# Turning 48 of the attention matrices by DVE squares and DMAs through DRAM instead of by PE

## The chip, the cores and the metric

The kernel runs on one core of a Trainium2 chip. The core has a matrix engine (PE; its weight loads are listed as PEld), a vector engine (DVE), an activation engine (ACT), a general engine (POOL), and a queue engine (SP) that here only issues DMAs. DMAs run on 16 DMA engines. The engines work in parallel, each in the order of its own instruction stream, and wait for each other on semaphores. The metric is the time of one execution on the device in microseconds (us), lower is better; the median of several runs is given.

## What is computed

Attention that keeps the 32 largest scores of each row, then an MLP with exact GELU on its output, all in float32:

```python
B, H, S, D = 8, 8, 576, 64
scores = scale * np.matmul(q, k.transpose(0, 1, 3, 2))          # (B, H, S, S)
kth = np.partition(scores, -32, axis=-1)[..., -32:-31]
scores = np.where(scores >= kth, scores, -1e9)
attn = np.exp(scores - scores.max(-1, keepdims=True))
attn = attn / (attn.sum(-1, keepdims=True) + 1e-9)              # P
x = np.matmul(attn, v)                                          # then (B*S, H*D) = (4608, 512)
h = x @ w_in                                                    # (4608, 2048)
g = 0.5 * h * (1.0 + erf(h / sqrt(2)))
return g @ w_out                                                # (4608, 512)
```

## The kernel before

**Items.** The heads are taken in pairs: 8 batches with 4 pairs each. An item is 128 query rows of one pair of heads (both heads side by side, `e` = 0 and 1), or, for the 64 rows left over at the end of a sequence, the last rows of two pairs (`t == NM`, a last-row item). Each batch has 16 main items and 2 last-row items, so there are N = 144. Main items come in twos: an even item and the odd one behind it are neighbouring 128-row tiles of the same pair of heads. Two batches make a ring of 36 items.

**The tile of an item.** `S_of[i]` is a 128 x 1152 tile, called s in the profile: 576 keys of head 0 and 576 keys of head 1. Its columns are ordered as 4 blocks of 128 keys of head 0, the last 64 keys of head 0 and those of head 1 next to each other, and 4 blocks of 128 keys of head 1: nine blocks of 128. Scores, the mask, the exponentials and the normalised P all live in this tile, one after the other. There are six such buffers.

**The loop.** The main loop runs a step n for each item and works on several items at once. In step n:

- PE computes scores (L371) and keys' ends (`last_keys`, L334) of items ahead; ACT copies them to s (L379, L342).
- PE multiplies P of the item pair that is finished with v (`attend(n - 3)`, L654, only when n - 3 is odd, since it takes 256 columns: an even item and the odd one behind it). ACT copies the result to xT (L659).
- PE turns over P of item n - 2 (`transposes(n - 2)`): one transpose for the 64 + 64 last keys (`tails`, L562) and eight for the blocks of both heads (`both`, `turn_over`, L592); ACT copies these to the tile pt (L572, L606).
- Between all these, PE runs pieces of the MLP of tokens that are ready (`mlp`: L712 is the first layer, L800 to L856 the second). `left[0]` says how many pieces a step gets.
- ACT applies mask and exponential to item n - 1 (`softmax`, L500 and L512), with the table loads that a change between GELU and exp needs, and GELU to the MLP's first layer (L728).
- DVE finds the 32nd largest score of each row of item n (`top_k`): four rounds of MAX8 and MATCH_REPLACE8. Rounds 0 and 1 run over 288 columns (the larger of two halves), rounds 2 and 3 over 576. The last thing in the step is the reciprocal of the sums of item n - 1 (`inverse`, L487).
- POOL prepares the lists for the top-k (L432, L440), adds the small constant to the sums (L493), multiplies P of item n - 1 by the reciprocals (`normalise`, L535) and adds up parts of the MLP.

An even step has the scores of two items, `attend` and an even item's transposes; an odd step has an odd item's transposes. From item 9 on P is normalised in place by POOL (`DIAGS`); before that PE multiplies by a diagonal matrix as it transposes.

**The tile pt.** It is one buffer of 128 keys x 9 blocks x 256 columns. Columns 0 to 127 hold the turned P of the even item, 128 to 255 that of the odd item. In the kernel before, blocks 0 to 3 are head 0, 4 to 7 head 1, and 8 the last keys of both.

**Queues.** SP's instruction stream holds the loads of q and k (L109, for pairs from the second batch's on 8 DMAs per load, in runs of 32 columns, so that DVE can turn them over in 32 x 32 squares, L269 to L273), the loads of v (L116, L119) and the stores of the output (`store`, L779). A DMA that has to wait holds up all DMAs behind it on SP. DMAs that read or write the raw tiles wait for the engine that uses them.

**An order written out by hand.** The scheduler is off (`manual_schedule`): the order of each engine's instructions is the order in which the loop issues them. The lines around the change:

```python
product = attend(n - 3)
...
tr = transposes(n - 2)
...
if few[0]:
    now, tr, prep = tr + prep[:1], [], prep[1:]
for x, piece in enumerate(now):
    piece(n + 2 if few[0] else None)
    ready[0] = n_tok[0]
    if few[0] and x == 2:
        break
    mlp(1)
```

`few[0]` holds from step 13 on. `SINGLE` is range(18, 28): items whose top-k runs all rounds over 576 columns, since POOL is busy with the weights then.

Of the kernel before, what the change touches and what calls it, by code (L numbers as in the profile page):

```python
# [8 lines left out]
TOPK = 32  # L9
# [5 lines left out]
def kernel(  # L15
# [19 lines left out]
    nc = tc.nc  # L35
# [5 lines left out]
    B, H, S, D = q.shape  # L41
# [19 lines left out]

    const = ctx.enter_context(tc.tile_pool(name="const", bufs=1))
    work = ctx.enter_context(tc.tile_pool(name="work", bufs=2))
    ps = ctx.enter_context(tc.tile_pool(name="ps", bufs=2, space=bass.MemoryType.PSUM))
    ctx.enter_context(tc.manual_schedule())

# [24 lines left out]
    def raw_of(n, pair):  # L91
        if n != "v":
            return raws[n][pair % 2 if pair < SQUARES else 0]
        return raws[n][pair % len(raws[n])]

    def load(n, pair, queue=None, queue2=None):
        if pair >= n_pairs:
# [341 lines left out]
            both, top = lists_of[i][:, :, 1].bitcast(i32), lists_of[i][:, :, 0].bitcast(i32)  # L439
            nc.gpsimd.tensor_tensor(into_of(i)[:, :, 1].bitcast(i32), both, top, op=ALU.subtract)  # L440

    def top_k(i, last):


        stat_of[i] = st = {
            "first": work.tile([P, 2, 8], f32, tag="first", name="first"),
            "neg": work.tile([P, 2], f32, tag="neg", name="neg"),
            "bias": work.tile([P, 2], f32, tag="bias", name="bias"),
            "den": work.tile([P, 2], f32, tag="den", name="den"),
            "rden": work.tile([P, 2], f32, tag="rden", name="rden"),  # L450
        }
        top = work.tile([P, 2, TOPK - 8], f32, tag="top", bufs=1, name="top")
        into = [st["first"]] + [top[:, :, 8 * r : 8 * r + 8] for r in range(TOPK // 8 - 1)]
        if paired(i):
            t = lists_of[i]
            u = into_of(i)
            both = u.rearrange("p e h n -> p e (h n)")
            rounds = [(t[:, :, 0], u[:, :, 0]), (u[:, :, 0], u[:, :, 0])]
            rounds = [(*(rounds[r] if 16 * r < TOPK else (both, both)), x) for r, x in enumerate(into)]
        else:  # L460
            s = S_of[i].rearrange("p (e n) -> p e n", e=2)
            t = work.tile([P, 2, S], f32, tag="lists", name="rest")
            rounds = [(s if r == 0 else t, t, x) for r, x in enumerate(into)]
        for r, (src, dst, x) in enumerate(rounds):
            for e in range(2):
                nc.vector.max(x[:, e], src[:, e])  # L466
            if r < len(rounds) - 1:
                for e in range(2):
                    nc.vector.match_replace(dst[:, e], x[:, e], src[:, e], LOWEST)  # L469
            if r == len(rounds) - 1:  # L470
                last()

        st["kth"] = top[:, :, TOPK - 9]
# [64 lines left out]
    pt_end = const.tile([P, 2, P], f32, name="pt_end")  # L538
    nc.gpsimd.memset(pt_end, 0.0)

    def transposes(i):

        if i < 0 or i >= N:
            return []
        t, s = items[i][1], S_of.pop(i)
        diag = diag_of.pop(i, None)

        def tails(ahead):
            tp = bank("tp_t")
            keys = last_keys(ahead, tp) if ahead is not None and ahead < N else None  # L550
            at = P
            if t % 2 == 0:
                pt_now[0] = work.tile([P, 2 * NM + 1, 2 * P], f32, tag="pt", bufs=1, name="pt")
            if diag is not None:
                for e in range(2):
                    nc.tensor.matmul(
                        tp[e * TL : (e + 1) * TL, at : at + P],
                        lhsT=s[:, SM + e * TL : SM + (e + 1) * TL], rhs=diag[:, e],
                        start=True, stop=True,
                    )  # L560
            elif t < NM:
                nc.tensor.transpose(tp[:, at : at + P], s[:, SM : S + TL], ident)  # L562
            else:
                for r in range(2):
                    nc.tensor.transpose(
                        tp[0:TL, at + r * P : at + (r + 1) * P],
                        s[:, r * S + SM : (r + 1) * S], ident,
                    )
            if keys:
                keys()  # L570
            if t < NM:
                nc.scalar.copy(  # L572
                    out=pt_now[0][:, 2 * NM, t % 2 * P : (t % 2 + 1) * P], in_=tp[:, at : at + P]
                )
                return
            for e in range(2):
                c = slice(e * TL, (e + 1) * TL)
                nc.scalar.copy(
                    out=halves(pt_end[c, 0, :], e, P),
                    in_=halves(tp[0:TL, at : at + 2 * P], e, P),  # L580
                )

        x = t % 2 * P if t < NM else 0

        def turn_over(tp, e):
            first = e * (S + TL if t < NM else S)
            for j in range(NM):
                to, part = tp[:, j * P : (j + 1) * P], s[:, first + j * P : first + (j + 1) * P]
                if diag is not None:
                    nc.tensor.matmul(to, lhsT=part, rhs=diag[:, e], start=True, stop=True)  # L590
                else:
                    nc.tensor.transpose(to, part, ident)  # L592

        def main(e):
            tp = bank("tp")
            turn_over(tp, e)
            nc.scalar.copy(  # L597
                out=pt_now[0][:, e * NM : (e + 1) * NM, x : x + P],
                in_=tp.rearrange("p (j n) -> p j n", j=NM),
            )  # L600

        def both():
            tp = pair_tile("tp")
            for e in range(2):
                turn_over(tp[:, e], e)
            nc.scalar.copy(  # L606
                out=pt_now[0][:, 0 : 2 * NM, x : x + P],
                in_=tp.rearrange("p e (j n) -> p (e j) n", j=NM),
            )

        if few[0]:
            return [tails, lambda _: both()]
        return [tails] + [lambda _, e=e: main(e) for e in range(2)]
# [21 lines left out]
    def attend(i):  # L635

        if i < 0 or i >= N:
            return False
        pair, t = items[i]
        b, at = divmod(pair, NP)  # L640
        if t < NM and t % 2 == 0:
            return False
        pt = pt_now[0]
        o = bank("o")
        n, row = (2 * P, (t - 1) * P) if t < NM else (TL, SM)
        tok = place_of(b, row)
        gap = RING if t == NM else COLS if tok % RING >= COLS else RING - COLS
        assert read[0] >= tok - gap + n
        c = slice(column(tok), column(tok) + n)
        if t < NM:  # L650
            vt = raw_of("v", pair)
            for j in range(NJ):
                for e in range(2):
                    nc.tensor.matmul(  # L654
                        o[e * D : (e + 1) * D, 0:n], lhsT=vt[:, j, e, :],
                        rhs=pt[:, e * NM + j if j < NM else 2 * NM, :],
                        start=(j == 0), stop=(j == NJ - 1),
                    )
            copies.append(lambda: nc.scalar.copy(out=xT[:, at, c], in_=o[:, 0:n]))  # L659
        else:  # L660
            for r in range(2):
                vt = raw_of("v", pair + r)
                for j in range(NJ):
                    for e in range(2):
                        nc.tensor.matmul(  # L665
                            o[e * D : (e + 1) * D, r * TL : (r + 1) * TL], lhsT=vt[:, j, e, :],
                            rhs=pt[:, r * NM + j, half(r, e)] if j < NM else pt_end[:, r, half(r, e)],
                            start=(j == 0), stop=(j == NJ - 1),
                        )
            copies.append(lambda: nc.scalar.copy(  # L670
                out=xT[:, at : at + 2, c],
                in_=o[:, 0 : 2 * TL].rearrange("p (r n) -> p r n", r=2),
            ))

        if t == (NM if b % 2 == 0 else NM - 1):
            for r in range(2 if t == NM else 1):
                load("v", pair + r + NP)
        if at == (NP - 1 if t < NM else NP - 2):
            assert n_tok[0] == tok
            n_tok[0] = tok + n  # L680
        return True
# [85 lines left out]
    def store(tok, y):  # L767

        lo = 0
        while lo < P:  # L770
# [5 lines left out]
            )  # L776
            m = min(end - at, P - lo)
            row += (2 * two + b) * S
            nc.sync.dma_start(out=out[row : row + m, :], in_=y[lo : lo + m])  # L779
            lo += m  # L780

    def acc_tile(x):
# [297 lines left out]
    ahead = N + 4  # L1080
    for n in range(ahead):

        left[0] = room_in(n)
        few[0] = n > START + 2
        eager[0] = n > N
# [88 lines left out]
        mlp(left[0])  # L1174
        run_gelus()
        if n < N:
            top_k(n, lambda: inverse(n - 1))
            if n == 0:
                larger(1)
        else:  # L1180
# [59 lines left out]
```

## Time and profile before

| | |
|---|---|
| median of 3 runs | 1522.78 us (1522.46 to 1523.19) |
| the profiled execution | 1522.78 us, its span 1520.8 us |
| granted TensorE clock | 1.0 |
| DMA packets | 195017, of which 185888 are under 512 bytes |
| SP's DMA queue | 193616 packets, 54.14 MB, 15.2% of the 16 engines' time |
| HBM | 45.08 MB read, 9.44 MB written |

The profile is of one execution. Rows of a group read: line, engine, operation, output and input tiles, shapes, count, then busy time, mean ns of one, and the idle time of the engine just before these instructions with what ended it. Rows of the timeline read: start, duration, engine, line, operation, count, and in brackets the idle time before it with what ended it. Rows of a window read: start and end, length, busy time and count for PE, PEld, DVE, ACT and POOL, granted clock, share of the DMA engines and GB/s. Rows of DMA issues read: tiles, queue, operation, count, size of each and median us from issue to landing; queue rows in the same view read: packets, MB, share of the 16 engines' time.

### The profile page before, as it was taken

How to read it: one execution, taken by the hardware profiler on the slowest of the kernel's cores; microseconds unless marked ns; L12 is line 12 of the kernel's file. 1: busy time of each engine (PE TensorE's matmuls, PEld its weight loads, DVE VectorE, ACT ScalarE, POOL GpSimd, SP SyncE). 2: the span in 40 equal slices, each digit the busy share in tenths (PEclk: the TensorE clock that was granted, in tenths of full speed). 3: DMA queues.
4: the chain of work that ended last, by engine and by line, in shares of the span. 5: the costliest groups of instructions: out<-in, count | busy, mean ns of one | idle time of the engine just before them, and what ended most of it. 6: DMA issues, size and time to landing. Idle time of an engine off the chain costs nothing.

```text
span 1520.8 us, 26952 instructions
## 1 busy us (share of the span) xinstructions
PE 1506.9 (99%) x9249; PEld 1191.2 (78%) x9249; DVE 1235.6 (81%) x3270; ACT 1155.1 (76%) x2038; POOL 1137.0 (75%) x1291
## 2 busy tenths in 40 slices
PE   8999999999999999999999999999999999999999
PEld 6776678877878778877888778887787877887887
DVE  7999899988888878888888887888888887887701
ACT  7999877777877777777877778787777777787730
POOL 6877667777878868777787978776787886877742
PEclk9999999999999999999999999999999999999999
DMA  7425310111101210012201111011110111000000
GB/s 200 135 84 125 85 35 1 31 35 30 36 9 24 45 34 15 1 31 49 38 14 24 31 28 42 1 30 31 32 31 16 24 31 32 15 1 15 8 14 15
DMA packets 195017, 56.28 MB, mean 37 GB/s; under 512 B 185888, under 2 KB 186432, under 8 KB 194880
## 3 DMA queue, kind: packets, MB, share of 16 engines
q1 hardware_dynamic: 193616, 54.14, 15.2%
q8 instruction: 73, 1.20, 0.3%
q14 instruction: 64, 0.52, 0.1%
q10 hardware_dynamic: 1200, 0.39, 0.1%
q0 software_dynamic: 64, 0.03, 0.0%
HBM read 45.08 MB, written 9.44 MB: 36 GB/s over the span
## 4 chain that ended last, share of the span: by engine, by line
PE 94%; ACT 0%; DVE 0%; issue 0%; POOL 0%; DVEq 0%
PE h_ps L712 34%; PE y_ps L856 20%; PE o L654 9%; PE tp L592 8%; PE s_ps L371 7%; PE seven L854 3%; PE y_ps L818 2%; PE y_ps L800 2%; PE y_ps L821 2%; PE tp_t L334 2%; PE o L665 1%; PE s_ps L386 1%; PE tp_t L562 1%; PE tp_t L348 0%; PE warm L1040 0%; PE tp L590 0%
## 5 line engine op out<-in xcount | busy, mean ns | idle before, releaser
L712 PE MATMUL h_ps<-xT,w_in_sb 128*128 128x256 f32 (+1 forms) x2560 | 544.0, 361 | 0.0
L712 PEld LDWEIGHTS h_ps<-xT,w_in_sb 128*128 128x128 f32 x2560 | 433.7, 191 | 70.9 <-issue 25.2
L466 DVE MAX8 top<-lists 128x8 f32<-128x576 f32 (+1 forms) x792 | 477.6, 643 | 0.1
L469 DVE MATCH_REPLACE8 lists<-top,lists 128x288 f32<-128x288 f32 (+1 forms) x528 | 307.7, 588 | 0.0
L535 POOL TENSOR_TENSOR s<-s,rden 128x1152 f32<-128x1152 f32 x135 | 285.8, 2117 | 0.3 <-DVE rden L487 0.3
L493 POOL TENSOR_SCALAR den<-den 128x2 f32<-128x2 f32 x144 | 31.3, 218 | 283.4 <-ACT s L512 281.5
L512 ACT ACTIVATE s<-s,bias 128x576 f32<-128x576 f32 x288 | 224.6, 783 | 10.7
L500 ACT ACTIVATE s<-s,neg 128x576 f32<-128x576 f32 x288 | 225.6, 791 | 0.0
L606 ACT COPY pt<-tp 128x1024 f32<-128x1024 f32 x133 | 135.1, 1016 | 111.0 <-PE tp L592 111.0
L487 DVE RECIPROCAL rden<-den 128x2 f32<-128x2 f32 x144 | 23.8, 165 | 210.4 <-POOL den L493 209.9
L440 POOL TENSOR_TENSOR lists<-lists 128x576 int32<-128x576 int32 x132 | 186.2, 1411 | 4.0
L432 POOL TENSOR_TENSOR lists<-s 128x576 int32<-128x576 int32 x133 | 187.0, 1406 | 0.0
L654 PEld LDWEIGHTS o<-pt,raw_v 128*64 128x64 f32 x1280 | 86.5, 136 | 85.8 <-issue 44.3
L654 PE MATMUL o<-pt,raw_v 128*64 128x256 f32 x1280 | 152.9, 384 | 0.7 <-ACT pt L597 0.4
L856 PE MATMUL y_ps<-w_out_sb,sum 128*128 128x256 f32 x472 | 140.4, 379 | 0.0
L592 PE MATMUL tp<-ident,s 128*128 128x128 f32 x1080 | 140.1, 273 | 0.0
L592 PEld LDWEIGHTS tp<-ident,s 128*128 128x128 f32 x1080 | 126.4, 141 | 14.5 <-issue 1.9
L379 ACT ACTIVATE s<-s_ps 128x1024 f32<-128x1024 f32 x127 | 125.0, 1031 | 9.6 <-PE s_ps L371 9.5
L371 PE MATMUL s_ps<-kt,qm 64*128 64x512 f32 x512 | 129.4, 618 | 0.8 <-ACT s L377 0.8
L469 DVE MATCH_REPLACE8 lists<-first,lists 128x288 f32<-128x288 f32 x264 | 114.2, 438 | 0.0
L856 PE MATMUL y_ps<-w_out_sb,g 128*128 128x256 f32 x480 | 113.4, 379 | 0.0
L728 ACT ACTIVATE g<-h_ps 128x512 f32<-128x512 f32 x144 | 78.2, 595 | 42.1 <-PE h_ps L712 41.5
(163 smaller groups left out, 2516.1 us busy)
## 6 DMA issues: line engine op xcount, KB each, us to landing
raw_v<-in_v_dram SPq DMA_DIRECT2D x64, 128.0 KB, 2.4
out_dram<-y SPq DMA_DIRECT2D x30, 256.0 KB, 2.0
raw_q<-in_q_dram SPq DMA_DIRECT2D x112, 64.0 KB, 2.0
raw_k<-in_k_dram SPq DMA_DIRECT2D x112, 64.0 KB, 2.0
w_out_sb<-in_moe_w_in_dram SPq DMA_DIRECT2D x14, 511.8 KB, 4.7
w_out_sb<-in_moe_w_out_dram SPq DMA_DIRECT2D x10, 511.8 KB, 4.3
w_sum<-in_moe_w_out_dram SPq DMA_DIRECT2D x6, 511.8 KB, 4.2
raw_q<-in_q_dram SPq DMA_DIRECT2D x112, 8.0 KB, 1.8
```

The source lines that it names most:

```text
L371: nc.tensor.matmul(s_ps[:, e], lhsT=q_t[rows, :], rhs=kt[rows, 0:SM], start=True, stop=True)
L432: nc.gpsimd.tensor_tensor(t[:, :, 1].bitcast(i32), a.bitcast(i32), b.bitcast(i32), op=ALU.add)
L440: nc.gpsimd.tensor_tensor(into_of(i)[:, :, 1].bitcast(i32), both, top, op=ALU.subtract)
L466: nc.vector.max(x[:, e], src[:, e])
L469: nc.vector.match_replace(dst[:, e], x[:, e], src[:, e], LOWEST)
L500: nc.scalar.activation(s, s, func=AF.Prelu, bias=st["neg"][:, e : e + 1], scale=1.0, alpha=STEEP)
L512: nc.scalar.activation(s, s, func=AF.Exp, bias=st["bias"][:, e : e + 1], scale=1.0, accum_out=st["den"][:, e : e + 1],)
L535: nc.gpsimd.tensor_tensor(s, s, wide, op=ALU.mult)
L592: nc.tensor.transpose(to, part, ident)
L654: nc.tensor.matmul(o[e * D : (e + 1) * D, 0:n], lhsT=vt[:, j, e, :], rhs=pt[:, e * NM + j if j < NM else 2 * NM, :], start=(j == 0), stop= ...
L712: nc.tensor.matmul(h_tile(u)[:, i, :], lhsT=w_in_sb[:, ko, f * P : (f + 1) * P], rhs=xT[:, ko, c0 : c0 + n], start=(ko == 0), stop=(ko == ...
L856: nc.tensor.matmul(acc[names][:, k], lhsT=lhsT, rhs=rhs, start=(j == 0 and k == 0), stop=(j == FT // 2 - 1 and k == 1),)
```

## The change

For an item that `squared(i)` names, PE no longer turns P over and ACT no longer copies it. Instead:

- In step i + 2, DVE transposes the whole tile s in place, ahead of round 2 of that step's top-k (`middle`, `square_p`). This turns over each 32 x 32 square where it stands.
- After that step's top-k, SP issues four DMAs that write s to a DRAM tile, 32 rows each, in runs of 32 numbers (`write_p`). The order in DRAM puts the squares where the full transpose has them. The loads of v and stores of the output that come up earlier in that step are held back and issued behind these (`issue`, `flush`).
- At the start of step i + 3, SP issues four DMAs that load the first half of pt, 32 rows each, in runs of 128 numbers (`read_p`).
- PE still does the keys' ends of an item ahead at the place of the transposes (`keys_only`).

The nine blocks in pt now have the order that they have in s (head 0, last keys, head 1), so `attend`, `tails`, `main` and `both` address them accordingly; this holds for all items. The diff, cut:

```diff
+    dram = ctx.enter_context(tc.tile_pool(name="dram", bufs=2, space=bass.MemoryType.DRAM))
...
+    held, late_issues = [False], []
+    def issue(f):
+        if held[0]:
+            late_issues.append(f)
+        else:
+            f()
+    def flush():
+        held[0] = False
+        while late_issues:
+            late_issues.pop(0)()
...
-    def top_k(i, last):
+    def top_k(i, last, middle):
...
         for r, (src, dst, x) in enumerate(rounds):
+            if 16 * r == TOPK:
+                middle()
...
+    def squared(i):
+        return SINGLE.stop - 2 < i < N - 2 and i % 2 == 0 and items[i][1] < NM and i % RINGS != 12
+    RINGS = 2 * len(items) // B
+    turned = {}
+    def square_p(i):
+        if squared(i):
+            s = S_of[i]
+            nc.vector.transpose(s, s)
+    def write_p(i):
+        if squared(i):
+            turned[i] = d = dram.tile([SQ, NJ + NM, P // SQ, P], f32, tag="turned", name="turned")
+            s = S_of.pop(i).rearrange("p (x j) -> p x j", j=SQ)
+            d = d.rearrange("i c k n -> i (c k) n")
+            for a in range(P // SQ):
+                rows = slice(a * SQ, (a + 1) * SQ)
+                nc.sync.dma_start(out=d[:, :, rows], in_=s[rows])
+    def read_p(i):
+        if squared(i):
+            d = turned.pop(i)
+            for k in range(P // SQ):
+                nc.sync.dma_start(
+                    out=pt_now[0][k * SQ : (k + 1) * SQ, :, 0:P], in_=d[:, :, k, :]
+                )
     def transposes(i):
         if i < 0 or i >= N:
             return []
+        if squared(i):
+            def keys_only(ahead):
+                pt_now[0] = work.tile([P, 2 * NM + 1, 2 * P], f32, tag="pt", bufs=1, name="pt")
+                if ahead is not None and ahead < N:
+                    last_keys(ahead, bank("t_ps"))()
+            return [keys_only]
...
-                    out=pt_now[0][:, 2 * NM, t % 2 * P : (t % 2 + 1) * P], in_=tp[:, at : at + P]
+                    out=pt_now[0][:, NM, t % 2 * P : (t % 2 + 1) * P], in_=tp[:, at : at + P]
...
+            pt = pt_now[0][:, 0, x : x + P]
             nc.scalar.copy(
-                out=pt_now[0][:, 0 : 2 * NM, x : x + P],
-                in_=tp.rearrange("p e (j n) -> p (e j) n", j=NM),
+                out=bass.AP(
+                    tensor=pt.tensor, offset=pt.offset,
+                    ap=[list(pt.ap[0]), [NJ * 2 * P, 2], [2 * P, NM], [1, P]],
+                ),
+                in_=tp.rearrange("p e (j n) -> p e j n", j=NM),
             )
...
-                        rhs=pt[:, e * NM + j if j < NM else 2 * NM, :],
+                        rhs=pt[:, e * NJ + j if j < NM else NM, :],
...
-                load("v", pair + r + NP)
+                issue(lambda r=r: load("v", pair + r + NP))
...
-            nc.sync.dma_start(out=out[row : row + m, :], in_=y[lo : lo + m])
+            to, part = out[row : row + m, :], y[lo : lo + m]
+            issue(lambda to=to, part=part: nc.sync.dma_start(out=to, in_=part))
...
     for n in range(ahead):
+        held[0] = n < N and squared(n - 2)
+        read_p(n - 3)
...
-            top_k(n, lambda: inverse(n - 1))
+            top_k(n, lambda: inverse(n - 1), lambda: square_p(n - 2))
+            write_p(n - 2)
+            flush()
```

`SINGLE.stop - 2` is 26 and `RINGS` is 36, so `squared` names the even main items from 28 to 140 without 48, 84 and 120: 48 items.

More of the change, by code (lines that the diff above doesn't have):

```diff
@@ L597, in main @@
             nc.scalar.copy(
-                out=pt_now[0][:, e * NM : (e + 1) * NM, x : x + P],
+                out=pt_now[0][:, e * NJ : e * NJ + NM, x : x + P],
                 in_=tp.rearrange("p (j n) -> p j n", j=NM),
@@ L666, in attend @@
                             o[e * D : (e + 1) * D, r * TL : (r + 1) * TL], lhsT=vt[:, j, e, :],
-                            rhs=pt[:, r * NM + j, half(r, e)] if j < NM else pt_end[:, r, half(r, e)],
+                            rhs=pt[:, r * NJ + j, half(r, e)] if j < NM else pt_end[:, r, half(r, e)],
                             start=(j == 0), stop=(j == NJ - 1),
```

## The prediction

> **What bounds the kernel now.** I read the page's busy line and chain first, then the groups by line and form, then one pair of steps in the timeline.
>
> ```profile
> PE 1506.9 (99%) x9249; PEld 1191.2 (78%) x9249; DVE 1235.6 (81%) x3270; ACT 1155.1 (76%) x2038; POOL 1137.0 (75%) x1291
> PE 94%; ACT 0%; DVE 0%; issue 0%; POOL 0%; DVEq 0%
> PE h_ps L712 34%; PE y_ps L856 20%; PE o L654 9%; PE tp L592 8%; PE s_ps L371 7%; PE seven L854 3%; PE y_ps L818 2%; PE y_ps L800 2%; PE y_ps L821 2%; PE tp_t L334 2%; PE o L665 1%; PE s_ps L386 1%; PE tp_t L562 1%; PE tp_t L348 0%; PE warm L1040 0%; PE tp L590 0%
> ```
>
> The chain that sets the end is PE's own instruction stream for 94% of the span: work taken off PE shortens the kernel for as long as nothing else becomes the limit. P's transposes (L592, L562) are 9% of it. The groups give their counts, and DVE's wait at the end of each step:
>
> ```profile
> L592 PE MATMUL tp<-ident,s 128*128 128x128 f32 x1080 | 140.1, 273 | 0.0
> L562 PE MATMUL tp_t<-ident,s 128*128 128x128 f32 x119 | 33.3, 280 | 0.0
> L487 DVE RECIPROCAL rden<-den 128x2 f32<-128x2 f32 x144 | 23.8, 165 | 210.4 <-POOL den L493 209.9
> ```
>
> The mean of one transpose is no price, because matmuls are pipelined; the price is the distance from a start to the next instruction's start. Here is the pair of steps 70 and 71, in the part of the kernel that the change reaches:
>
> ```profile
> 699.81 2.38 PE L654 MATMUL o<-pt,raw_v 128*64 128x256 f32 x20
> 700.05 2.10 POOL L535 TENSOR_TENSOR s<-s,rden 128x1152 f32<-128x1152 f32 x1
> 703.11 1.40 DVE L466 MAX8 top<-lists 128x8 f32<-128x576 f32 x2
> 705.04 0.27 PE L562 MATMUL tp_t<-ident,s 128*128 128x128 f32 x1
> 705.15 1.03 PE L712 MATMUL h_ps<-xT,w_in_sb 128*128 128x256 f32 x4
> 706.01 1.04 PE L592 MATMUL tp<-ident,s 128*128 128x128 f32 x8
> 706.88 3.62 PE L712 MATMUL h_ps<-xT,w_in_sb 128*128 128x256 f32 x16
> 707.09 1.01 ACT L606 COPY pt<-tp 128x1024 f32<-128x1024 f32 x1 [1.31 <-PE tp L592]
> 708.80 0.78 ACT L512 ACTIVATE s<-s,bias 128x576 f32<-128x576 f32 x1
> 710.01 0.17 DVE L487 RECIPROCAL rden<-den 128x2 f32<-128x2 f32 x1 [2.72 <-POOL den L493]
> 718.99 0.17 DVE L487 RECIPROCAL rden<-den 128x2 f32<-128x2 f32 x1 [0.16 <-POOL den L493]
> 719.60 2.38 PE L654 MATMUL o<-pt,raw_v 128*64 128x256 f32 x20
> ```
>
> The pair lasts 719.60 - 699.81 = 19.79 us. DVE idles 2.72 us in the even step: ACT's second exp comes behind its copy of the transposed P, that copy waits for PE, and DVE's reciprocal waits for the exp. In the odd step DVE idles only 0.16 us. So PE is the bound, and DVE is close to it.
>
> **The change, part by part.** By the condition in `squared`, the even items from 28 to 140 that are no last-row items, without 48, 84 and 120, go the new way: 48 of them (the one-line summary says 49; one more would be worth 1 us).
>
> *Removed.* PE: the eight L592 from 706.01 to 706.88, 0.87 us, and the L562 from 705.04 to 705.15, 0.11 us: 0.98 us per item, 48 x 0.98 = 47.0 us. By the chain's rounded shares (8% and 1% of 1520.8 us over 1080/8 = 135 items and 119 tails) it is 1.03 us, or 49 us. ACT loses the 1.01 us copy, its wait of 1.31 us and the copy of the tail; that brings the second exp, and so DVE's reciprocal, earlier in even steps, and is no term of its own. The keys' matmul (L334) stays. `attend` reads pt in another order of its nine blocks and `both` copies with one stride more: nothing for either, since count and size stay the same and ACT has room.
>
> *Added on DVE.* One 128x1152 transpose in place, ahead of round 2 of the top-k. Smaller ones stand in the trace:
>
> ```profile
> L269 DVE STREAM_TRANSPOSE kt<-raw_k 128x640 f32<-128x640 f32 x28 | 23.3, 830 | 0.0
> L273 DVE STREAM_TRANSPOSE qm<-raw_q 128x512 f32<-128x512 f32 x28 | 18.8, 672 | 0.0
> L271 DVE STREAM_TRANSPOSE kt<-raw_q 128x128 f32<-128x128 f32 x28 | 8.1, 291 | 0.2 <-DMA raw_q<-in_q_dram 0.2
> ```
>
> From 128 to 640 columns is 539 ns, 1.05 ns a column, so 1152 columns take 830 + 512 x 1.05 = 1.37 us. As bounds I take 0.83 us (the widest seen) and the 2.10 us of POOL's pass over the same tile. The transpose waits for P to be normalised; that ended at 700.05 + 2.10 = 702.15, and round 2 started at 703.11, so it finds P ready by 0.96 us. Whether DVE has the 1.37 us is read from windows, each from one reciprocal's end to another's: a ring of 36 steps, a short pair, the pair above, a pair with two loads of q and k to turn over.
>
> ```profile
> 486.85:848.71 361.86, 361.85 (x2218) 287.57 (x2217) 303.67 (x817) 280.10 (x500) 285.34 (x323) 1.00 0.13 27
> 579.90:598.04 18.14, 18.14 (x130) 15.53 (x130) 16.18 (x45) 14.41 (x27) 14.57 (x16) 1.00 0.00 1
> 699.20:718.99 19.79, 19.79 (x112) 15.68 (x110) 16.91 (x46) 15.17 (x27) 14.56 (x16) 1.00 0.19 35
> 738.78:758.61 19.83, 19.83 (x112) 16.24 (x110) 17.71 (x48) 16.05 (x32) 15.25 (x17) 1.00 0.26 46
> ```
>
> The fourth number is DVE's busy time, the second PE's. Over the ring, with 15 new items, DVE needs 303.67 + 15 x 1.37 = 324 us and PE 361.86 - 15 x 0.98 = 347 us. In the pair above it is 18.28 against 18.81 us. Only in the tight pairs does DVE pass PE: 19.08 against 18.85, and 17.55 against 17.16 us. Those pairs lose 0.23 to 0.39 us; with about four of them in each of three rings that is 3.5 us. Without any cover the 48 transposes would cost 66 us, more than PE gains.
>
> *Added on SP's queue.* Four stores of 32 rows each (36 x 32 packets of 128 bytes, 1152 a store, 288 on each of the 16 DMA engines for the four) once the transpose is done; then, at the start of the next step, four loads that wait until all has landed (32 x 9 packets of 512 bytes each). No store of short packets is in the trace. The nearest rows are, in this order, a window with loads of 128-byte packets, one with stores of 2-KB packets and one with loads of 256-byte packets:
>
> ```profile
> q1 hardware_dynamic: 2432, 0.30, 28.0%
> raw_k<-in_k_dram SPq DMA_DIRECT2D x4, 64.0 KB, 1.9
> ...
> q1 hardware_dynamic: 288, 0.52, 45.6%
> out_dram<-y SPq DMA_DIRECT2D x2, 256.0 KB, 2.2
> ...
> q1 hardware_dynamic: 1216, 0.30, 34.4%
> raw_v<-in_v_dram SPq DMA_DIRECT2D x2, 128.0 KB, 2.3
> ```
>
> The windows last 6.5, 3.0 and 3.8 us, so a packet takes 0.280 x 16 x 6.5 / 2432 = 12 ns, 0.456 x 16 x 3.0 / 288 = 76 ns, and 0.344 x 16 x 3.8 / 1216 = 17 ns. From 12 to 17 ns for 128 bytes more is some 0.04 ns a byte, by which 2 KB would take about 88 ns: a store costs per byte what a load does. So for a stored packet of 128 bytes I take 12 ns, with 76 ns as the far bound, and for a loaded one of 512 bytes 27 ns. Landing: a 64-KB load (32 packets an engine, 0.4 us) lands 1.9 us after issue, 1.5 us of which is not data. The stores: 1.5 + 288 x 12 ns = 5.0 us. The loads: four issues, at the pace of these rows (eight issues in 3.87 us, 0.48 each), the last 1.45 us after the first and landing like v's after 2.3 us: 3.75 us. With 0.1 us for each of the two wake-ups, C = 9.0 us from transpose to landed.
>
> ```profile
> 711.63 3.87 SPq L109 DMA_DIRECT2D raw_k<-in_k_dram  x8
> 720.67 4.31 SPq L109 DMA_DIRECT2D raw_q<-in_q_dram  x8
> 723.69 1.40 DVE L466 MAX8 top<-lists 128x8 f32<-128x576 f32 x2
> 738.53 1.30 PE L654 MATMUL o<-pt,raw_v 128*64 128x256 f32 x10
> 701.78 0.39 SPq L116 DMA_DIRECT2D raw_v<-in_v_dram  x1
> 702.79 0.58 SPq L116 DMA_DIRECT2D raw_v<-in_v_dram  x1
> ```
>
> The time there is: round 2 starts at 703.11, the transpose ends at 704.48, and the next `attend` would start at 719.60 - 0.98 = 718.62: 14.1 us. In the next pair, a tight one, 723.69 + 1.37 to 738.53 - 0.98: 12.5 us. So 3.5 to 5 us are to spare, and the stores and loads cost nothing; the cover is the step and a half between the halves of an item pair. If it is gone, lateness x costs half of x per pair, because the loop that closes (P lands, `attend`, the rest of the step, ACT's exp, DVE's reciprocal, top-k, transpose of the item after next) spans two pairs.
>
> *Moved.* Behind the waiting store on SP stand v's loads and the output's stores of that step (now issued after it); behind the waiting load stand the next step's loads of k and q. q's eight issues of an even step come ahead of the store and end at 724.98, when that transpose would end at 725.06: no delay. k's start at 711.63, and P's loads would be issued from 704.48 + 5.1 to 711.5, so k hardly moves. v is needed a batch later, and a y buffer has far more than these 5 us. Nothing for these. The loads write one half of the columns of pt while ACT writes the other; v's two halves interleave likewise in one tile, and the second was issued 1.01 us after the first, before that could land after 2.3 us: no wait between halves.
>
> [...]
>
> **The sum.** The profiled execution took 1522.78 us, which is also the median (its span is 1520.8, with 2 us around it): 1522.8 - 47.0 + 3.5 = 1479 us.
>
> **Rivals.**
>
> *P comes late, and it costs more than PE gains.* Place: the first L654 of even steps waits for DMA. It turns slower when C passes about 13.3 + 2 x 0.98 = 15.3 us, that is when a stored 128-byte packet takes over 12 + 6.3 / 0.288 = 34 ns. At 40 ns C is 17.1 us, late by 3.8, 1.9 a pair, 48 x 1.9 = 91 us: 1570 us. At the far bound of 76 ns: C = 27.4, 7.05 a pair, 1817 us. For it: no short store in the trace, and all of them go through 32 rows at a time. Against it: stores and loads lie on one line of time over bytes.
>
> *P comes a little late.* At 29 ns C is 13.9 us, 0.6 late, 0.3 a pair: 1493 us.
>
> *DVE becomes the bound.* Its gap in the pair above is 19.79 - 16.91 = 2.88 us; a transpose of that length, or waits for P around it, leaves the pair as long as before: 1523 us. Against it: three rows on one line for the transpose. At POOL's 2.10 us it would still be some 1490.
>
> *The freed PE time isn't filled,* because the MLP's pieces now follow each other without transposes between them and meet ACT's gelu or a single PSUM bank; or the loads and ACT's copies into pt do wait for each other. Half the gain: 1501 us. Against it: L712 and L854 have no idle time now, and ACT gets freer.
>
> [...]
>
> **How the numbers follow.** Forecast 0.55; P too late 0.20; a little late 0.11; DVE the bound 0.09; not filled 0.05. A run of this kernel tells about 0.2%, 3 us, from no change. Faster: 0.55 + 0.11 + 0.05 and a little of DVE's = 0.73; same 0.04 (the rest of DVE's case near zero); slower 0.23. The range goes from 1470 (1.03 us per item and no tight pairs lost, with a few us over) to 1570, the middle of the late case; beyond lies about a tenth above and less below. The forecast's own range is 1470 to 1490.
>
> **What would show it.** L592 x696 and L562 x71; 48 transposes of 128x1152 near 1.37 us; DVE's wait before L487 falling from 210 us to under 150; PE still at 98 to 99%; the stores of 144 KB landing within some 5 us; DMA packets up by 48 x 5760 = 276,000. A wait of L654 for the DMA of pt of over 2 us a pair makes the prediction wrong, and so do idle gaps of PE behind POOL's L535 in odd steps.

## The result, and the profile after

The changed kernel takes 1565.06 us in the median (1564.13 to 1566.77), the kernel before 1522.72 us in the same comparison: a ratio of 1.0279, with a 95% interval of 1.0261 to 1.0297. It is slower by 42 us. The profiled execution took 1564.7 us, its span is 1562.9 us.

The page's busy line, the clock and the chain of the changed kernel:

```profile
PE 1484.1 (95%) x8817; PEld 1160.6 (74%) x8817; DVE 1294.8 (83%) x3318; ACT 1099.3 (70%) x1942; POOL 1140.3 (73%) x1291
PEclk9999999999999999999999999999999999999999
PE 7%; DMA 1%; POOL 1%; ACT 1%; SPq 1%; DVE 0%; issue 0%; DVEq 0%; ACTq 0%
```

PE has 432 matmuls fewer, but it now has idle time: its busy share fell from 99 to 95%. The clock line rounds to 9 everywhere; the mean granted clock is 0.978. The chain, followed back, accounts for little over a tenth of the span here, so it says little; the waits say more. From the groups by line and form:

```profile
L649 PE MATMUL tp<-ident,s 128*128 128x128 f32 x696 | 90.4, 273 | 0.0
L619 PE MATMUL tp_t<-ident,s 128*128 128x128 f32 x71 | 20.2, 285 | 0.5 <-POOL s L552 0.5
L569 DVE STREAM_TRANSPOSE s<-s 128x1152 f32<-128x1152 f32 x48 | 65.5, 1364 | 0.0
L504 DVE RECIPROCAL rden<-den 128x2 f32<-128x2 f32 x144 | 23.3, 162 | 193.5 <-POOL den L510 193.1
L715 PE MATMUL o<-pt,raw_v 128*64 128x256 f32 x1280 | 173.6, 422 | 64.7 <-DMA pt<-turned 64.0 <-ACT pt L654 0.4 <-ACT pt L664 0.2
```

The transposes went as announced (696 and 71 left, 48 new ones on DVE of 1.36 us). The last row is where the time went: the multiplication with v waits 64.0 us for the loads of P, where it had 0.7 us of idle time before. And its own busy time grew from 152.9 to 173.6 us for the same 1280 matmuls.

The views of the waits, first those of the engines, then those of SP's queue (who waited for whom, us in total, times, longest):

```profile
PE o L715 <- DMA pt<-turned: 64.0, 14, 6.3
...
SPq L841 <- POOL y L979: 247.1, 14, 89.0
SPq L579 <- DVE s L569: 202.5, 35, 16.8
SPq L586 <- DMA turned<-s: 76.8, 48, 3.9
```

Only 14 of the 48 items are waited for, but for up to 6.3 us each. One of them, in the timeline of DVE, SP, POOL and PE:

```profile
779.66 1.37 DVE L569 STREAM_TRANSPOSE s<-s 128x1152 f32<-128x1152 f32 x1
781.09 3.25 SPq L579 DMA_DIRECT2D turned<-s  x4
793.26 0.73 POOL L979 TENSOR_TENSOR y<-y,y 128x256 f32<-128x256 f32 x1
794.01 1.06 SPq L841 DMA_DIRECT2D out_dram<-y  x2
795.29 2.54 SPq L586 DMA_DIRECT2D pt<-turned  x4
800.65 3.98 PE L715 MATMUL o<-pt,raw_v 128*64 128x256 f32 x20 [5.47 <-DMA pt<-turned]
```

P's stores go out as soon as DVE is done, at 781.09. Then SP does nothing for nearly ten microseconds: the next DMA in its order is a store of the MLP's output, and its data come from POOL (L979), which gets to them at 793.26. P's loads stand behind that store and start at 795.29; they take 5 us, and PE waits 5.47 us. There is a second kind:

```profile
696.32 1.36 DVE L569 STREAM_TRANSPOSE s<-s 128x1152 f32<-128x1152 f32 x1
700.31 1.16 SPq L841 DMA_DIRECT2D out_dram<-y  x2
701.51 4.18 SPq L124 DMA_DIRECT2D raw_k<-in_k_dram  x8
705.81 3.38 SPq L579 DMA_DIRECT2D turned<-s  x4
```

Here an output store that came up at the end of the step before, and k's loads behind it, stand ahead of P's stores, which start 8.1 us after the transpose's end. Nine of the 14 waits are of the first kind (41.6 us together) and four of the second (21.4 us). The last, of 1.06 us, has loads of v between P's stores and P's loads.

The granted clock around this second one (start and end, length, five busy times with counts, clock, DMA share, GB/s):

```profile
711.00:715.20 4.20, 1.03 (x6) 0.19 (x2) 3.85 (x14) 1.95 (x3) 4.02 (x5) 1.00 0.57 137
715.20:722.00 6.80, 4.13 (x20) 2.49 (x20) 5.50 (x10) 0.00 (x0) 4.62 (x6) 0.50 0.67 123
722.00:728.00 6.00, 6.00 (x30) 5.16 (x29) 0.51 (x2) 4.55 (x9) 0.68 (x3) 1.00 0.71 133
```

PE idles from 712.04 to 717.87, and from 715.2 to 722.0 it is granted half its clock: the multiplication behind the wait takes 4.4 instead of 2.4 us. The half clock begins 3.2 us into the idle time and ends 4.1 us behind it. A wait of 2.16 us was followed by half the clock too (last section).

The balance: 1522.8 less 47.0 for the transposes, plus 64.0 of waiting, 173.6 - 152.9 = 20.7 at the half clock, and 3.5 where DVE is short makes 1564.0, against 1564.7 measured. The last term was only forecast so far; a run below measures it.

### The profile page after: what moved, and what is told of

Its sections match the earlier page's. It is cut to its first block, busy times and chain, and to the rows that moved or that the text cites. A ratio compares the mean times of both kernels' runs of the same rounds, so it can differ in the third digit from the quotient of the medians.

```text
span 1562.9 us, 27012 instructions
## 1 busy us (share of the span) xinstructions
PE 1484.1 (95%) x8817; PEld 1160.6 (74%) x8817; DVE 1294.8 (83%) x3318; ACT 1099.3 (70%) x1942; POOL 1140.3 (73%) x1291
## 5 line engine op out<-in xcount | busy, mean ns | idle before, releaser
L773 PE MATMUL h_ps<-xT,w_in_sb 128*128 128x256 f32 (+1 forms) x2560 | 537.1, 362 | 0.1
L715 PE MATMUL o<-pt,raw_v 128*64 128x256 f32 x1280 | 173.6, 422 | 64.7 <-DMA pt<-turned 64.0
L715 PEld LDWEIGHTS o<-pt,raw_v 128*64 128x64 f32 x1280 | 99.4, 150 | 156.0 <-issue 97.5
L664 ACT COPY pt<-tp 128x1024 f32<-128x1024 f32 x85 | 86.5, 1018 | 62.0 <-PE tp L649 62.0
L720 ACT COPY xT<-o 128x256 f32<-128x256 f32 x64 | 24.3, 380 | 147.9 <-PE o L715 147.9
L483 DVE MAX8 first<-lists 128x8 f32<-128x288 f32 x268 | 106.4, 436 | 0.0
```

The source lines that it names most:

```text
L715: nc.tensor.matmul(o[e * D : (e + 1) * D, 0:n], lhsT=vt[:, j, e, :], rhs=pt[:, e * NJ + j if j < NM else NM, :], start=(j == 0), stop=(j = ...
L773: nc.tensor.matmul(h_tile(u)[:, i, :], lhsT=w_in_sb[:, ko, f * P : (f + 1) * P], rhs=xT[:, ko, c0 : c0 + n], start=(ko == 0), stop=(ko == ...
```

## The experiments

Theory A: P is late only where SP's queue stands, because an output store that waits for POOL is ahead of P's stores or between P's stores and P's loads. Theory B: the DMA path as such is too slow for the time there is.

**Output stores issued by POOL**

```diff
-            issue(lambda to=to, part=part: nc.sync.dma_start(out=to, in_=part))
+            nc.gpsimd.dma_start(out=to, in_=part)
```

> One edit to the changed kernel: the stores of the output are issued by POOL, which computes them, instead of by SP. Theory A (P comes late only where SP's queue stands: an output store ahead of P's stores or between P's stores and P's loads waits for POOL's sum, and everything behind it on SP waits too): 13 of the 14 waits of L654's matmul for the DMA of pt go or shrink to what q's and k's loads leave, 64 us of waiting becomes under 12 us, the half-clock stretches mostly go, and the time falls from 1565 to 1480-1495 us. Theory B (the DMA path itself is too slow: 128-byte stores, landing times or the DMA engines' load): the stores are 0.25 MB each and few, so the waits stay, 1555-1570 us.

1499.84 us (ratio to before 0.9852, 0.9838 to 0.9867). The waits for P are gone but for 1.1 us before the last attend, which speaks against B; but the time is above the range. The wait view of this run shows why:

```profile
PEld tp_t L619 <- POOL s L552: 19.5, 13, 2.2
PE tp_t L619 <- POOL s L552: 17.1, 11, 2.0
```

POOL now spends time on issuing (38 stores; the one at 488.64 us takes 0.63 us), comes later to normalising P, and the odd items' transposes on PE wait 17.1 us for it; in the next run, where SP issues the stores, this row has 1.5 us. A blocked queue was cleared by loading an engine that had no time there.

**Another order on SP alone**

```diff
-        held[0] = n < N and squared(n - 2)
         read_p(n - 3)
+        if not squared(n - 2):
+            flush()
+        held[0] = squared(n - 2) or squared(n - 1)
...
             write_p(n - 2)
-            flush()
```

Stores of the output and v's loads are issued only behind P's loads.

> The changed kernel with another order on SP alone: output stores and v's loads are issued only behind P's loads, in odd steps, never ahead of P's stores or between stores and loads. Nothing else moves. Theory A: as with POOL's queue, no output store blocks P, 1478-1492 us; what is left are q's loads ahead of P's stores (up to 4 us, within the slack of most pairs). Theory B: 1555-1570 us. If the held stores make POOL or ACT wait for a y buffer, some tens of us stay.

1480.25 us (0.9722, 0.9708 to 0.9737): the slowdown of 42 us is gone and as much again is gained, with every engine doing what it did. The page's busy line, two groups, and the same item as above in the timeline:

```profile
PE 1461.5 (99%) x8817; PEld 1147.6 (78%) x8817; DVE 1294.3 (88%) x3318; ACT 1099.9 (74%) x1942; POOL 1140.9 (77%) x1291
...
L715 PE MATMUL o<-pt,raw_v 128*64 128x256 f32 x1280 | 153.0, 384 | 2.6 <-ACT s L529 1.1 <-DMA pt<-turned 0.8 <-ACT pt L654 0.4
L504 DVE RECIPROCAL rden<-den 128x2 f32<-128x2 f32 x144 | 23.1, 160 | 110.1 <-POOL den L510 109.0
...
744.79 1.36 DVE L569 STREAM_TRANSPOSE s<-s 128x1152 f32<-128x1152 f32 x1
746.22 3.29 SPq L579 DMA_DIRECT2D turned<-s  x4
752.31 2.55 SPq L586 DMA_DIRECT2D pt<-turned  x4
758.95 1.06 SPq L841 DMA_DIRECT2D out_dram<-y  x2
760.25 2.38 PE L715 MATMUL o<-pt,raw_v 128*64 128x256 f32 x20
```

P's loads follow as soon as the stores have landed, the output's store comes behind, and PE doesn't wait. It is back at 99%, the multiplication with v at 153.0 us and thus at full clock. DVE's wait in front of the reciprocal fell from 210 to 109 us.

**Only one of the two positions cleared**

```diff
-        if not squared(n - 2):
-            flush()
-        held[0] = squared(n - 2) or squared(n - 1)
+        flush()
+        held[0] = squared(n - 2)
```

(against the run before)

> Half of the reordering on SP: output stores and v's loads of the step in which P is stored go behind P's loads, but a store that comes up at the end of the odd step before still stands ahead of P's stores. Theory A: the nine waits in which the store stood between P's stores and P's loads go, the three in which P's stores were 8 us late behind a store and k's loads stay, at 5.8 us and some 2 us of half clock each: 1497-1510 us, about 22 us over the run with both positions cleared. If one position alone made everything late: 1478-1484 or 1550-1565 us.

1506.94 us (0.9897, 0.9881 to 0.9914), 26.7 us over the run with both cleared, and four waits are left:

```profile
PE o L715 <- DMA pt<-turned: 20.5, 4, 5.9
```

Three of them are the expected ones, at 341, 697 and 1053 us, 5.3 to 5.9 us each; a fourth of 4.0 us stands at 1405 us, where P's stores start late too. So both positions matter, and each wait costs its length and, with the mean clock at 0.992, some 1.5 us more.

**q's and k's loads behind P's loads too**

```diff
-                load("q", pair + ahead)
+                issue_even(lambda: load("q", pair + ahead))
```

(and the same for k; `issue_even` puts a load of an even step on the same list)

> As the run before, and the loads of q and k that come up in an even step are issued behind P's loads as well. Theory A: the last waits for P go: 1476-1488 us, and 0 to 6 us less than the run before. If q or k then comes late for its squares on DVE, a wait of DVE for raw_q or raw_k appears and the time is above the run before.

1483.71 us (0.9745, 0.9729 to 0.9761): within the range, but 3.5 us worse and not better. Its wait view has the new wait that was named:

```profile
DVE kt L295 <- DMA raw_q<-in_q_dram: 3.7, 4, 1.7
```

q's loads ahead of P's stores cost nothing; late q's cost a little.

**The idle time filled**

```diff
+        if n in FILL:        # 34, 42, 50, 70, 78, 86, 106, 114, 122
+            warm = bank("warm")
+            for _ in range(26):
+                nc.tensor.matmul(warm[:, 0:P], lhsT=ident, rhs=ident, start=True, stop=True)
         product = attend(n - 3)
```

> The changed kernel with 26 matmuls on the identity (about 2.9 us of PE work, nobody reads them) ahead of attend in 9 of the 14 steps in which PE waits 5 to 6 us for P. They fit into the waits, so the waits end at the same time. If the idle time itself lowers PE's granted clock (half speed was granted for 3.4 to 6.8 us from these waits on, and attend took up to 4.5 instead of 2.4 us), the clock stays at 1.00 there and 10 to 25 us of the 1565 go: 1540-1555 us. If the clock has nothing to do with the waits, 1563-1568 us.

1547.24 us (1.0163, 1.0148 to 1.0178): 468 matmuls that nobody reads (the trace has two for each of the 9 x 26 in the program) make the changed kernel 17.8 us faster. The groups show where:

```profile
L716 PE MATMUL o<-pt,raw_v 128*64 128x256 f32 x1280 | 155.6, 389 | 14.6 <-DMA pt<-turned 12.6 <-issue 1.1 <-ACT pt L655 0.4
L1171 PE MATMUL warm<-ident 128*128 128x128 f32 x468 | 54.6, 277 | 0.0
```

The busy time of the multiplication falls by 18.0 us to 155.6, and the mean clock is 0.997. So that share of the loss came from the clock and not from the DMAs.

**Without DVE's transpose**

```diff
-            nc.vector.transpose(s, s)
+            return
```

> The version with both positions cleared (1480 us), without DVE's transpose of s: P of the 48 items isn't turned within its squares. Everything else, the DMAs too, is as in that version. If DVE's 1.37 us lie beside PE's work but for the tight pairs: 1475-1480 us, 1 to 5 us less. If DVE had become the bound of most pairs: below 1470 us.

1476.72 us (0.9698, 0.9684 to 0.9712), 3.5 us less than with it. That is the price of 48 x 1.36 = 65 us on DVE: all but 3.5 us lie beside PE's work. Where it is lost shows in the distances from one multiplication with v to the next in the two traces: six pairs, two in each ring, lose 0.37 to 0.60 us, 2.7 us together; two more lose 1.0 us, most of it in waits for P of 0.2 and 0.7 us; and the last pair loses 1.7 us. The stretches ahead of the 48 items and behind the last pair differ by 1.7 us the other way. And 1522.5 - 1476.7 = 45.8 us is what the transposes cost on PE, to the extent that nothing else waits.

**P stored twice**

```diff
+            other = dram.tile([SQ, NJ + NM, P // SQ, P], f32, tag="other", name="other")
+            other = other.rearrange("i c k n -> i (c k) n")
-            for a in range(P // SQ):
...
+            for to in (other, d):
+                for a in range(P // SQ):
```

> The version with both positions cleared (1480 us), with P stored twice, first to another DRAM tile, then to the one that is read. From transpose to landed it takes 11.2 to 13 us there; four more stores make it 14.8 to 16.5, against 12.5 to 14.5 us that are to be had, so P is 1 to 3 us late in nearly every pair. If lateness costs half of itself per pair, as the prediction has it: 1505-1530 us. If it costs all of itself: 1535-1590 us. If DMAs of short packets cost nothing in this kernel whatever their number: 1480 us.

1589.86 us (1.0442, 1.0424 to 1.0461): 110 us more than with one store, above what the half rule was to give, and at the upper edge of what full lateness was to give.

```profile
L718 PE MATMUL o<-pt,raw_v 128*64 128x256 f32 x1280 | 175.0, 424 | 84.0 <-DMA pt<-turned 80.1 <-DMA out_dram<-y 3.1 <-ACT pt L657 0.4
```

PE waits 81 us longer than with one store, and 175.0 - 153.0 = 22 us go to the half clock (the mean clock is 0.981), which neither case had counted. That doesn't refute the half rule, because P is also later than expected: it has landed 15.3 to 21.6 us after the transpose. Take as due the moment, counted from the transpose's end, at which the multiplication with v starts in the version with both positions cleared. By the landing times in the two traces, P is then late in 47 of the 48 items, by 154 us in all, and PE idles 84 us for it, 0.55 of the lateness: where nearly every item is late, two pairs do share it. In the changed kernel, by the same reckoning, P is late by 69 us and PE idles 65 us for it: a late item whose neighbours are on time is paid for almost in full. In both, the clock comes on top.

**All 51 items**

```diff
-        return SINGLE.stop - 2 < i < N - 2 and i % 2 == 0 and items[i][1] < NM and i % RINGS != 12
+        return SINGLE.stop - 2 < i < N - 2 and i % 2 == 0 and items[i][1] < NM
```

> The version with both positions cleared (1480 us), with items 48, 84 and 120 turned in the new way too, 51 in all. By 0.98 us each less on PE, less what DVE lacks in those pairs (DVE idles only 0.37 us in their even step): 1477-1480 us. If the loads of k and q that come up in their odd step and are needed in the next are held up behind P's loads: 1481-1490 us.

1496.93 us (0.9830, 0.9816 to 0.9845): 16.7 us for three items, more than either case. The wait view:

```profile
DVE kt L286 <- DMA raw_q<-in_q_dram: 9.0, 3, 3.3
PE tp_t L619 <- POOL s L552: 12.0, 5, 4.2
```

In the odd step behind these items k and q are loaded and needed in the next step. Behind P's loads they come 3 us late, DVE waits for them three times, POOL's normalising and PE's transposes wait for DVE, and with waits of about 4 us PE loses clock again (0.994 in the mean). The place and the mechanism were named, the price was too low.

## Why the prediction was wrong

*The step that failed* is the one called "Moved". It asked what stands behind P's DMAs on SP and who waits for that, and answered rightly that nobody waits for v or y. It did not ask what stands ahead of P's loads between them and P's stores, nor what was left over from the step before; for q's and k's loads alone it looked ahead. C was summed as if SP were free at every moment. Where it says "Nothing for these", the changed kernel lost 64.0 us in waits and 20.7 us at the half clock; with both positions cleared the time is 1480.25 us, with only one of them 1506.94 us. The trace of before had the row that speaks of it, in the view of SP's waits:

```profile
SPq L779 <- POOL y L917: 527.4, 14, 88.9
```

There an output store holds SP for 38 us in the mean, and it costs nothing, because nothing behind it is urgent: from 296.53 to 1440.36 us PE is busy for 1143.81 of 1143.83 us. With P's loads behind it, it decides. In the timeline above SP waits for 9.7 us, from 784.3 to 794.0, for the data of such a store, and P's loads, which stand behind it, are issued from 795.29 on.

*The half clock* is in no part of the prediction: 20.7 us. The trace of before could not show it in these steps: from 296.53 to 1440.36 us PE idles for 0.02 us in all, and its clock is 1.00. The prediction priced idle time of PE at its length.

*What was right*, now measured with SP's order mended: PE's gain was put at 47.0 us and is 45.8; DVE's shortage at 3.5 us and is 3.5; the sum at 1479 us, and the mended order takes 1480.25. That the 3.5 agrees so well is in part luck: it was argued from about four tight pairs in each of three rings, and the traces show two in each, 2.7 us in all, and besides them waits for P and the last pair. A transpose was put at 1.37 us and takes 1.36. The stored packet of 128 bytes was put at 12 ns. The queue rows of the mended run, in a window with P's four stores (6.1 us) and one with its loads (5.7 us):

```profile
q1 hardware_dynamic: 4672, 0.59, 63.5%
turned<-s SPq DMA_DIRECT2D x4, 144.0 KB, 3.5
...
q1 hardware_dynamic: 1216, 0.59, 37.3%
pt<-turned SPq DMA_DIRECT2D x4, 144.0 KB, 3.1
```

0.635 x 16 x 6.1 / 4672 = 13.3 ns a packet, and 0.373 x 16 x 5.7 / 1216 = 28 ns for the loads (27 forecast).

*A size that was off*: C. It was put at 9.0 us. Four stores are issued in 3.29 us (0.82 each and not 0.48; each has 1152 packets where the loads of k that the 0.48 came from have 512, but whether that is the reason isn't shown) and have landed 6.0 us after the first issue, not 5.0; the loads, landing 3.1 us after issue, take 5.2, not 3.75. The 0.1 us for a wake-up was an estimate; from the transpose's end to the first store's issue the timeline has 0.07 us. In the mended order C is 11.2 to 13.1 us, 11.8 in the median. Of the 3.5 us that a tight pair had to spare next to nothing is left: five of the 48 multiplications with v start within 0.2 us of P's landing, and three of these have waited. That it was still enough is luck.

*The rivals.* "P comes late" had the sign and the place (the multiplication with v waits for the DMA), but for a packet price that isn't there. The half price for lateness held about where nearly all items were late (0.55 with the doubled store), but the changed kernel's late items stand apart and were paid for almost in full; and it left out the clock. DVE did not become the bound, and PE's freed time was filled.

## What to carry to other kernels

Treat a DMA queue as an engine with an order (in the changed kernel one waiting store held P's loads for 9.7 us, and 14 waits for P cost 64.0 us): when a transfer that someone waits for is put on it, list every DMA that stands ahead of it and what that one waits for, above all stores of results that come late. Where such a store is the problem, move it behind the urgent transfer before moving it to another engine (1480.25 against 1499.84 us here). And price an idle stretch of PE of several microseconds at more than its length (here 20.7 us at the half clock came on top of the 64.0 us).

## What the runs showed of the hardware that was not expected

In the changed kernel PE idles nine times for 5.28 to 6.29 us, and with each of these idle times its granted clock goes to 0.50 for 3.4 or 6.8 us. With 26 useless matmuls in each of the nine the mean clock is 0.997 instead of 0.978, the multiplication with v is busy for 155.6 instead of 173.6 us, and the time is 17.8 us lower. Of the shorter waits one of 2.16 us is followed by a slow multiplication, and one of 2.31 us isn't; behind each row stand two windows, with PE's busy time as the second number and the clock as the seventh:

```profile
1045.19 3.52 PE L715 MATMUL o<-pt,raw_v 128*64 128x256 f32 x20 [2.16 <-DMA pt<-turned]
1042.85:1046.27 3.42, 1.26 (x12) 0.92 (x12) 3.42 (x12) 1.31 (x2) 3.42 (x4) 1.00 0.71 145
1046.27:1049.69 3.42, 3.42 (x16) 2.06 (x12) 3.42 (x9) 0.94 (x2) 2.04 (x2) 0.50 0.43 68
...
672.63 2.38 PE L715 MATMUL o<-pt,raw_v 128*64 128x256 f32 x20 [2.31 <-DMA pt<-turned]
670.81:674.22 3.41, 1.59 (x16) 1.32 (x18) 3.41 (x13) 0.64 (x1) 3.39 (x2) 1.00 0.62 112
674.22:677.64 3.42, 3.42 (x21) 2.68 (x18) 3.42 (x6) 1.91 (x4) 1.42 (x1) 1.00 0.41 66
```

The twelve half-speed stretches of this trace ahead of its end all start and end on one grid of 3.41 us, and the second wait is cut in two by a line of that grid. Every window of the grid that was at full clock and in which PE was busy for at most 0.37 of the time is followed by half the clock (12 windows), and none in which it was busy for 0.44 or more. This is read off one trace; no run was made to test the limit.

In the mended order the stores of P in runs of 128 bytes cost the DMA engines 13.3 ns a packet, close to the 12 ns of k's loads of that size in the trace of before.
